# Attention and routed experts on one core: two buffers for the loads, an order from a repeating table of times, and dummy products at twelve places

## The chip, the cores and the metric

The kernel runs on one NeuronCore of a Trainium2 chip. The metric is the time of one execution in microseconds of device time. Before the change the median of three runs is 1302.24 us (1299.56 to 1303.64).

## The reference

```
# q, k, v: (8 batches, 8 heads, 1152, 64), float32
q_pool = q.reshape(B, H, 576, 2, D).mean(axis=3)
scores = (q_pool @ k^T) / 8;  scores -= max over keys
attn = exp(scores) / (sum + 1e-9);  out = attn @ v          # (8, 8, 576, 64)
x = out.transpose(0, 2, 1, 3).reshape(4608, 512)
logits = x @ w_gate                                          # 8 experts
# greedy: go through all logits from the largest; give a token to an expert
# while the token is free and the expert holds fewer than 576 tokens
out[tokens of e] = relu(x[tokens of e] @ w1[e]) @ w2[e]
```

## The kernel before, in words

**Stages.** `attention()` works through 64 heads as 32 pairs (n = 0 to 31), two heads s = 0 and 1 of a pair after each other. `experts()` follows; it assigns the tokens and runs eight feed-forward blocks. The change lies in `attention()` alone.

**A head.** 1152 keys are nine blocks of 128, 576 pooled queries are the moving side. A step g is one key block of one head; a pair has 18. For each step the scores of 288 queries at a time are two products (L600 with the high parts, L601 with the low parts and the maxima) into one of three PSUM banks `sc`; ScalarE takes the exponential into `P` (L604; ten buffers); POOL, in five or six of 18 steps DVE, subtracts the high half of `P` from `P` and keeps the rest in `PM` (L607; ten buffers); and TensorE adds 15 small products (L617) into `av`. These are issued in groups of one or two steps. After nine steps DVE divides `av` and writes `X` (L639): one such evacuation ends each half of a pair.

**What a pair needs before its first scores.** SP loads `QD`, `KD`, `VD` (L389, L392, L396), of each of which there is one buffer. DVE sums query pairs into `QS` (L401), ScalarE sums absolute values into `VJ` (L406 for keys, L415 for queries), a few tiny DVE operations (L419 to L425) make scales, ScalarE writes the high halves `KH` (L440) and `QH` (L429; DVE at L431 for pair 0), DVE the low halves `KL` and `QL` (L442, L432), and SP copies all of them to `KA`, `KB`, `QA`, `QB` (L450) and `BD` (L436), which have two buffers each. The row maxima of the scores are estimated a pair ahead: 27 products (L497; L505 and L501 for pair 0) into the two double banks `mt`, reduced by DVE (`MX`, L524; for pair 0 partly through `MS`, L539 and L541), turned by TensorE (L554, L570) and written into `QB` (L558 and L561 for pair 0, `AU` and a DMA, L575, otherwise). `V` is split likewise (L466, L480, L483). After every second pair the gate is applied (L658, L661, L672, L676 or L678), and `X` is stored (L721).

**The order.** Every operation is put into a list by `add` with an engine, an estimated duration, what it reads and writes, and a due time. `Order.emit` is a list scheduler: it plays the engines forward with those durations and, among operations that are ready, takes the one with the lowest due time plus a lead from the table `LEAD`. What it yields is only an order: each engine runs its own sequence, waiting on semaphores. Small DVE and POOL operations that build tables for the experts (`routing_tables`, L254 to L292) are items of the same list.

**Warm-up.** 50 products of `ones` (L728) stand at the head of TensorE's sequence, and 65 more (L730) between the products of pair 0.

Of the kernel before, what the change touches and what calls it, by code (L numbers as in the profile page):

```python
# [1433 lines left out]
```

## Time and profile before

| | us |
|---|---|
| median of three runs | 1302.24 |
| the profiled execution | 1307.96 |
| its span, first to last instruction | 1306.2 |
| busy in the span: PE | 1247.8 |
| DVE | 1038.2 |
| POOL | 777.7 |
| ACT | 769.9 |

The profiled execution is 1.76 us longer than its span and 5.72 us longer than the median of the runs. PE is TensorE's products, PEld its weight loads, ACT ScalarE, POOL GpSimd, SP the engine that issues most DMAs. The ends of products are modelled and overlap, so a full PE is not PE at its peak; what one product costs is read from the starts of its row and of the next. The clock column is the share of 2.4 GHz that TensorE was granted; it knows two levels, 1.0 and 0.5.

### The profile page before, as it was taken

The numbers are of one execution on the slowest core, as the hardware profiler recorded it, in microseconds if no ns is written. First come the engines' busy times: TensorE is split into PE (matmuls) and PEld (weight loads), VectorE is DVE, ScalarE is ACT, GpSimd is POOL, SyncE is SP. The second block draws the span as 40 slices with busy tenths as digits, with TensorE's granted clock in tenths as the row PEclk, the third lists the DMA queues.
The fourth block names the chain that finished last, engine by engine and source line by source line (L and its number), as shares of the span: only waits on it lengthen the run. The fifth ranks groups of instructions, "written<-read, shape, count | busy, mean of one in ns | idle before, by whom it ended". The sixth has DMA issues, their size and how long they took to land.

```text
span 1306.2 us, 39238 instructions
## 1 busy us (share of the span) xinstructions
PE 1247.8 (96%) x15419; PEld 1008.1 (77%) x15419; DVE 1038.2 (79%) x2606; ACT 769.9 (59%) x1901; POOL 777.7 (60%) x746
## 2 busy tenths in 40 slices
PE   7899999999999999999999997799999999999996
PEld 4577787777777777777777776587978889798895
DVE  8999999999999999899999985898876767752120
ACT  4588777877877877877877864143333324334330
POOL 5275576565656656656657563257667667586631
PEclk8799999999999999999999998999999999999998
DMA  4655555654654654654655520225445343454301
GB/s 150 154 167 144 156 151 139 174 148 126 186 145 121 178 147 117 177 150 119 181 149 140 126 60 20 66 102 197 170 133 150 130 126 124 151 172 143 125 14 37
DMA packets 123541, 175.25 MB, mean 134 GB/s; under 512 B 49500, under 2 KB 86364, under 8 KB 121180
## 3 DMA queue, kind: packets, MB, share of 16 engines
q1 hardware_dynamic: 114876, 120.29, 34.2%
q0 software_dynamic: 8336, 52.44, 11.5%
q8 instruction: 121, 1.98, 0.7%
q14 instruction: 64, 0.52, 0.1%
q10 hardware_dynamic: 144, 0.02, 0.0%
HBM read 99.63 MB, written 18.87 MB: 91 GB/s over the span
## 4 chain that ended last, share of the span: by engine, by line
PE 72%; DVE 16%; issue 5%; DMA 4%; ACT 1%; SPq 1%; POOL 0%; POOLq 0%; DVEq 0%; ACTq 0%
PE ph L1327 16%; PE av L617 14%; PE po L1357 13%; PE mt L497 8%; PE sc L600 8%; PE sc L601 7%; DVE MX L524 4%; DVE PM L607 4%; DMA KA<-KL 2%; DMA KD<-in_kt_dram 1%; PE mt L658 1%; PE po L1354 1%; DVE KL L442 1%; DMA QA<-QH 1%; PE rt L1001 1%
## 5 line engine op out<-in xcount | busy, mean ns | idle before, releaser
L607 POOL TENSOR_TENSOR PM<-P 128x576 f16<-128x576 f32 x413 | 473.4, 1174 | 312.4 <-ACT P L604 263.8
L604 ACT ACTIVATE P<-sc 128x288 f32<-128x288 f32 x1152 | 396.1, 413 | 162.7 <-PE sc L601 151.4
L524 DVE TENSOR_REDUCE MX<-mt 128x2 f32<-128x768 f32 (+1 forms) x443 | 399.4, 919 | 47.1 <-PE mt L497 43.8
L600 PE MATMUL sc<-QA,KA 128*128 128x288 f16 x1152 | 309.9, 286 | 10.9 <-ACT P L604 8.9
L617 PEld LDWEIGHTS <-P 128*128 128x128 bf16 x5760 | 297.5, 98 | 27.8 <-issue 0.7
L601 PE MATMUL sc<-QB,KB 66*128 66x288 f16 (+1 forms) x1152 | 311.7, 288 | 0.6 <-DMA QB<-AU 0.4
L617 PE MATMUL av<-V,P 128*128 128x65 f16 (+1 forms) x5760 | 306.0, 193 | 1.2 <-DVE V L483 1.2
L617 PE MATMUL av<-V,PM 128*128 128x65 f16 x2880 | 296.4, 195 | 0.0
L617 PEld LDWEIGHTS <-PM 128*128 128x128 f16 x2880 | 265.4, 97 | 1.3 <-issue 1.3
L497 PE MATMUL mt<-KH,BD 128*128 128x384 f16 x837 | 200.2, 326 | 3.4 <-DVE MX L524 1.6
L1357 PE MATMUL po<-W2H,HX 128*128 128x512 f32 x512 | 168.2, 399 | 0.0
L601 PEld LDWEIGHTS <-KB 66*128 66x128 f16 (+1 forms) x1152 | 112.0, 97 | 66.7 <-issue 29.6
L1327 PE MATMUL ph<-XH,W1H 128*128 128x320 f32 (+1 forms) x512 | 153.0, 299 | 1.0 <-issue 0.5
L1327 PE MATMUL ph<-XL,W1H 128*128 128x320 f32 (+1 forms) x512 | 152.4, 298 | 1.6 <-DVE XL L1226 1.5
L1327 PE MATMUL ph<-XH,W1L 128*128 128x320 f32 (+1 forms) x512 | 152.3, 298 | 1.0 <-issue 1.0
L600 PEld LDWEIGHTS <-KA 128*128 128x128 f16 x1152 | 112.9, 98 | 49.5 <-issue 15.7
L1332 ACT ACTIVATE HX<-ph 128x256 fp32r<-128x256 f32 (+1 forms) x128 | 51.5, 413 | 134.0 <-PE ph L1327 125.5
L607 DVE TENSOR_TENSOR PM<-P 128x576 f16<-128x576 f32 x163 | 123.5, 767 | 6.4 <-ACT P L604 5.5
L1357 PE MATMUL po<-W2L,HX 128*128 128x512 f32 (+1 forms) x320 | 127.6, 399 | 0.0
L1336 DVE SCALAR_TENSOR_TENSOR HX<-ph,HX 128x256 fp32r<-128x256 f32 x128 | 52.9, 415 | 81.1 <-ACT HX L1332 77.6
L1357 PEld LDWEIGHTS po<-W2H,HX 128*128 128x128 f32 x512 | 95.3, 189 | 18.5 <-issue 1.7
L497 PEld LDWEIGHTS <-BD 128*128 128x128 f16 x837 | 75.3, 98 | 30.8 <-issue 10.4
(233 smaller groups left out, 1899.7 us busy)
## 6 DMA issues: line engine op xcount, KB each, us to landing
QD<-in_qt_dram SPq DMA_DIRECT2D x32, 576.0 KB
KD<-in_kt_dram SPq DMA_DIRECT2D x64, 288.0 KB
VD<-in_v_dram SPq DMA_DIRECT2D x32, 576.0 KB
QA<-QH SPq DMA_DIRECT2D x128, 72.0 KB
KA<-KH SPq DMA_DIRECT2D x64, 144.0 KB
KB<-KH SPq DMA_DIRECT2D x64, 144.0 KB
KA<-KL SPq DMA_DIRECT2D x64, 144.0 KB
x_dram<-X SPq DMA_DIRECT2D x16, 576.0 KB
```

What stands on the lines that cost most here:

```text
L442: od.add(t + 5 + 2 * z, "DVE", 727, lock=1, fn=lambda h=h: nc.vector.scalar_tensor_tensor(KL[0][:, h], KD[0][:, h], sk, KH[i][:, h], op0=O ...
L497: nc.tensor.matmul(out, BD[i][:, j], KH[i][:, ks], start=True, stop=True)
L524: od.add(t, "DVE", d, lambda: nc.vector.tensor_reduce(dst, src, axis=AX.X, op=OP.max), r=[mk], w=[("MX", i, j, c) for j, c in what], tag=" ...
L600: nc.tensor.matmul(c[:, :288], KA[i][:, s, ks], QA[i][:, s, qs], start=True, stop=False)
L601: nc.tensor.matmul(c[:, :288], KB[i][:kr, s, ks], QB[i][:kr, s, qs], start=False, stop=True)
L604: od.add(g + 0.1 + 0.01 * t, "ACT", 293, lambda c=c, qs=qs: nc.scalar.activation(p[:, qs], c[:, :288], AF.Exp, scale=1.0 / UNIT), r=[ck], ...
L607: od.add(g + 0.2, en, dur, lock=1, fn=lambda: eng.tensor_tensor(pm, p, hi, op=OP.subtract), r=[("P32", g % NP, 0), ("P32", g % NP, 1)], w= ...
L617: nc.tensor.matmul(out, w[:, qs], v, start=kb == 0 and j == 0 and y == 0, stop=kb == NKB - 1 and y == 2, skip_group_check=True)
L1327: nc.tensor.matmul(p, a[:, d, fs], b[:, d, qs], start=z == 0, stop=z == 11)
L1332: nc.scalar.activation(HH[:, f, qs], p, AF.Relu)
L1336: V.scalar_tensor_tensor(HL[:, f, 64 + 256 * hf:320 + 256 * hf], p[:, :256], 0.0, h[:, :256], op0=OP.max, op1=OP.subtract)
L1357: nc.tensor.matmul(o[:n], a[:, z, q0:q0 + n], b[:, z], start=z == 0 and y == 0, stop=z == 7, skip_group_check=True)
```

## The change

Three things, all in `attention()`:

1. `KD`, `QD`, `VD` get two buffers each; a pair uses those of number n % 2.
2. The list scheduler's forward play gives way to `Timed.emit`: an item's key is n times 23600 plus a number from the table `TIME`, found by the pair's own prefix (pairs 0 to 3, the last two as y and z) or else by e or o for even and odd pairs, and by the operation's name and count. Items are emitted by lowest key among those whose predecessors have been emitted. No durations enter. Which engine does what is unchanged.
3. Ahead of twelve items of pairs 0 to 2 on TensorE, `FILL` puts 7 to 45 products of `ones` (185 in all), into columns 384 to 511 of the first bank of `mt`.

```diff
+class Timed(Order):
+    def when(self, i):
+        n, name, t = self.names[i]
+        if name is None:
+            return -1e6
+        for p in ("0123" + "-" * self.pairs)[n] + ("yz"[n - self.pairs + 2] if n + 2 >= self.pairs else "-") + "eo"[n % 2]:
+            if p + name in self.table:
+                return n * self.period + self.table[p + name]
+        return t / NSTEP * self.period + self.period
+    def emit(self):
...
+        while heap:
+            _, i = heapq.heappop(heap)
+            for _ in range(FILL.get("%d%s" % self.names[items[i]][:2], 0)):
+                self.fill()
+            self.items[items[i]][4]()
...
+PERIOD = 23600
+FILL = {"0mm0a": 45, "0mm1b": 24, "0mm0b": 7, "0mmf": 12, "0wv0a": 9, "0mmi": 9, "0mm0d": 13, "0augtb": 11,
+        "0qkb4a": 13, "2mm0a": 9, "2mm2a": 9, "2mm3a": 24}
+TIME = {"0auga": -30939, "0augb": -19565, "0augta": -16763, "0augtb": -11483, "0av0a10a": 8356, "0av0a12a": 11915,
...
-    od = Order(LEAD, LATE)
...
+    od = Timed(TIME, PERIOD, npair)
+    od.fill = lambda: nc.tensor.matmul(mt[0][:, 0, 384:], ones, ones, start=True, stop=True)
...
-    KD = several(1, [128, S], F32, "KD")
-    QD = several(1, [128, 2, M], F32, "QD")
-    VD = several(1, [128, 2, NKB, D], F32, "VD")
+    KD = several(2, [128, S], F32, "KD")
+    QD = several(2, [128, 2, M], F32, "QD")
+    VD = several(2, [128, 2, NKB, D], F32, "VD")
...
+            od.add(t, "SP", 1200, lambda h=h: nc.sync.dma_start(KD[n % 2][:, h], kt[n][:, h]), w=[("KD", n % 2, z)],
```

What it moves, at two places. The first is the head of DVE's sequence, from the high half of pair 0's queries (`QH`) on. Before (line numbers of before; `MX0` and `KH0` belong to pair 0; `KS`, `KE` are the scales; `mt` the banks of the maxima):

```order
L431 TENSOR_SCALAR QH0_81<-QS0_112,KS0_102 128x576
L432 SCALAR_TENSOR_TENSOR QL0_83<-QS0_112,KS0_102,QH0_81 128x576
L442 SCALAR_TENSOR_TENSOR KL0_80<-KD0_109,KS0_102,KH0_78 128x576
L524 TENSOR_REDUCE MX0_119<-mt0_149 128x2
L442 SCALAR_TENSOR_TENSOR KL0_80<-KD0_109,KS0_102,KH0_78 128x576
L524 TENSOR_REDUCE MX0_119<-mt1_150 128x2
L524 TENSOR_REDUCE MX0_119<-mt0_149 128x2
L401 TENSOR_TENSOR QS0_112<-QD0_110 128x576
L539 TENSOR_TENSOR MS_118<-MS_118 128x5x192
L524 TENSOR_REDUCE MX0_119<-mt1_150 128x2
L539 TENSOR_TENSOR MS_118<-MS_118 128x5x96
L524 TENSOR_REDUCE MX0_119<-mt0_149 128x2
```

With the change (the numbers of lines differ by the added code; L717 is `KL`, L706 `QH`, L707 `QL`, L676 `QS`, L799 `MX`, and what ends in 1 belongs to pair 1):

```order
L717 SCALAR_TENSOR_TENSOR KL0_80<-KD0_109,KS0_102,KH0_78 128x576 x2
L700 TENSOR_SCALAR KS0_102<-KS0_102 128x1
L706 TENSOR_SCALAR QH0_81<-QS0_115,KS0_102 128x576
L707 SCALAR_TENSOR_TENSOR QL0_83<-QS0_115,KS0_102,QH0_81 128x576
L676 TENSOR_TENSOR QS0_115<-QD1_112 128x576
L799 TENSOR_REDUCE MX0_122<-mt1_153 128x2
L694 TENSOR_SCALAR KE1_105<-KS1_103 128x1
L696 TENSOR_SCALAR KE1_105<-KS1_103,KE1_105 128x1
L698 TENSOR_SCALAR KS1_103<-KE1_105 128x1
L799 TENSOR_REDUCE MX0_122<-mt0_152 128x2
L700 TENSOR_SCALAR KS1_103<-KS1_103 128x1
L717 SCALAR_TENSOR_TENSOR KL0_80<-KD1_110,KS1_103,KH1_79 128x576 x2
```

Both `KL` of pair 0 now stand ahead of its `QH`, and the sums, scales and `KL` of pair 1 stand between the maxima of pair 0. On SP, likewise, the keys of pair 1 are loaded ahead of the second half of the keys of pair 0, and on DVE the second `ndiag` (L373 before), which waits for POOL's last fill, stands ahead of pair 0's scales. The tables for the experts, which DVE built between the maxima of pair 0 (L267 to L292), now stand in pair 2 of its sequence.

The second place is SP's queue in the middle of the program, at the load of an odd pair's keys (`KD`), which is issued some three pairs ahead of their scores. Before:

```order
L436 DMA BD0_92<-QH0_81 64x9x64 x2
L392 DMA KD0_109<-in_kt_dram 128x576 x2
L450 DMA KB0_86<-KH0_78 64x1152
L450 DMA KA0_84<-KL0_80 64x1152
L450 DMA QA0_88<-QH0_81 64x576
L450 DMA KA0_84<-KH0_78 64x1152
L450 DMA QA0_88<-QH0_81 64x576
```

With the change, the same load, now to the second buffer:

```order
L850 DMA QB0_90<-AU_101 1x9x64 x2
L667 DMA KD1_110<-in_kt_dram 128x576 x2
L725 DMA KB1_87<-KH1_79 64x1152
L725 DMA QA1_89<-QH1_82 64x576
L725 DMA KA1_85<-KL0_80 64x1152
L725 DMA QA1_89<-QH1_82 64x576
```

The load stood behind the store of `X` and the copies `BD` of a pair and had to wait until the one buffer was read; now it stands right behind the copies of the maxima (`AU`) of the pair under way and goes to the buffer that is not being read. On ScalarE, the sum over it (`VJ` from `KD`) stands in the same half of the even pairs as before; in the odd pairs it has moved from the seventh step to the last two.

## Rows read from the trace of the kernel before

**Rows 1.** Busy time in four stretches: from the start to the first evacuation, the pairs in their regular turn, the last pairs, the experts. Columns: stretch (us), its length, busy us (instructions) of PE, PEld, DVE, ACT, POOL, granted clock, DMA share, GB/s.

```profile
0.00:53.30 53.30, 40.50 (x361) 27.55 (x362) 45.66 (x113) 28.35 (x64) 20.91 (x36) 0.74 0.53 154
...
107.00:753.30 646.30, 636.09 (x10224) 500.16 (x10223) 604.31 (x1125) 506.59 (x1296) 400.47 (x353) 1.00 0.55 148
753.30:806.00 52.70, 51.28 (x896) 41.71 (x894) 34.79 (x63) 32.01 (x87) 32.90 (x33) 1.00 0.17 44
806.00:1306.20 500.20, 469.55 (x3169) 400.07 (x3169) 301.58 (x1215) 162.06 (x353) 291.14 (x299) 0.97 0.37 121
```

**Rows 2.** DVE in order of time, the evacuation that ends a pair's first half: of pairs 0, 2, 3, 4, then of 20, 21 and 29. Columns: start, duration, engine, line, operation.

```profile
53.28 0.48 DVE L639 TENSOR_TENSOR X<-av,RS 128x320 f32<-128x320 f32 x1
...
106.99 0.47 DVE L639 TENSOR_TENSOR X<-av,RS 128x320 f32<-128x320 f32 x1
130.32 0.48 DVE L639 TENSOR_TENSOR X<-av,RS 128x320 f32<-128x320 f32 x1
154.57 0.48 DVE L639 TENSOR_TENSOR X<-av,RS 128x320 f32<-128x320 f32 x1
...
538.23 0.48 DVE L639 TENSOR_TENSOR X<-av,RS 128x320 f32<-128x320 f32 x1
563.82 0.48 DVE L639 TENSOR_TENSOR X<-av,RS 128x320 f32<-128x320 f32 x1
...
753.29 0.47 DVE L639 TENSOR_TENSOR X<-av,RS 128x320 f32<-128x320 f32 x1
```

**Rows 3.** Who waited for whom between 107 and 753.3 us: total us, times, longest.

```profile
ACT VJ L406 <- DMA KD<-in_kt_dram: 8.5, 8, 1.8
...
PE sc L600 <- ACT P L604: 6.6, 8, 1.1
```

**Rows 4.** PE in order of time in the regular turn, at four places where products follow each other without a wait: maxima, 30 weighted sums, six scores; then the gate's transposes and its products.

```profile
396.51 0.81 PE L497 MATMUL mt<-KH,BD 128*128 128x384 f16 x4
397.16 0.22 PE L617 MATMUL av<-V,P 128*128 128x65 f16 x2
...
398.07 0.49 PE L497 MATMUL mt<-KH,BD 128*128 128x384 f16 x2
...
399.30 0.28 PE L600 MATMUL sc<-QA,KA 128*128 128x288 f16 x1
...
400.05 0.22 PE L617 MATMUL av<-V,P 128*128 128x65 f16 x2
...
430.58 0.82 PE L658 MATMUL mt<-ident,X 128*128 128x128 f32 x6
...
437.84 0.83 PE L672 MATMUL mt<-XT,wgs 128*8 128x384 f32 x6
```

**Rows 5.** Busy time in three stretches of 5 us near the start, columns as in rows 1.

```profile
30.00:35.00 5.00, 2.42 (x11) 1.59 (x11) 4.00 (x15) 1.57 (x4) 1.45 (x3) 0.57 0.00 0
35.00:40.00 5.00, 3.15 (x12) 1.31 (x11) 4.93 (x12) 3.88 (x8) 0.89 (x1) 0.50 0.39 68
40.00:45.00 5.00, 3.76 (x47) 2.91 (x46) 4.97 (x7) 1.88 (x5) 0.00 (x0) 0.50 0.94 284
```

**Rows 6.** PE in order of time near the start: the first product of pair 0, a run of dummy products, and the last wait before the clock falls. In brackets: idle time before, and what ended it.

```profile
10.71 0.82 PE L505 MATMUL mt<-KH,QH 64*128 64x384 f16 x2 [3.61 <-DVE QH L431]
...
20.08 2.17 PE L730 MATMUL av<-ones 128*128 128x128 bf16 x33
...
32.58 0.16 PE L469 MATMUL mt<-VM,ones 128*128 128x1 bf16 x1 [3.63 <-DVE MX L524]
```

**Rows 7.** DVE in order of time near the start: the halves of queries and keys, maxima, a fold, the first `QB`, and one of the tables for the experts.

```profile
9.23 1.43 DVE L431 TENSOR_SCALAR QH<-QS,KS 128x576 f16<-128x576 f32 x1
10.69 0.82 DVE L432 SCALAR_TENSOR_TENSOR QL<-QS,KS,QH 128x576 f16<-128x576 f32 x1
11.43 0.81 DVE L442 SCALAR_TENSOR_TENSOR KL<-KD,KS,KH 128x576 f16<-128x576 f32 x1
...
13.75 1.81 DVE L524 TENSOR_REDUCE MX<-mt 128x2 f32<-128x768 f32 x2
...
16.15 0.65 DVE L539 TENSOR_TENSOR MS<-MS 128x960 bf16<-128x960 bf16 x1
...
22.41 0.69 DVE L558 SCALAR_TENSOR_TENSOR QB<-mt,ndiag 9x512 f16<-9x512 f32 x1 [1.27 <-PE mt L554]
...
26.54 1.80 DVE L276 TENSOR_SCALAR nib<-scratch 128x16 f32<-128x16 int32 x2
```

**Rows 8.** POOL in order of time: the last of the fills at the start.

```profile
10.40 0.38 POOL L364 MEMSET V<- 128x18 f16 x1
```

**Rows 9.** DVE's groups between 107 and 753.3 us that read two operands from SBUF, largest first: xcount, busy us, mean ns, idle before.

```profile
L607 DVE TENSOR_TENSOR PM<-P 128x576 f16<-128x576 f32 x135 | 100.6, 754 | 0.4
L483 DVE SCALAR_TENSOR_TENSOR V<-VD,VS,V 128x576 f16<-128x576 f32 x54 | 43.8, 810 | 0.0
L442 DVE SCALAR_TENSOR_TENSOR KL<-KD,KS,KH 128x576 f16<-128x576 f32 x54 | 41.8, 813 | 0.8 <-DMA QA<-QH 0.8
L432 DVE SCALAR_TENSOR_TENSOR QL<-QS,KS,QH 128x576 f16<-128x576 f32 x27 | 21.8, 807 | 0.0
L401 DVE TENSOR_TENSOR QS<-QD 128x576 f32<-128x576 f32 x26 | 19.5, 749 | 0.0
```

**Rows 10.** POOL's one group in the same stretch, columns as in rows 9.

```profile
L607 POOL TENSOR_TENSOR PM<-P 128x576 f16<-128x576 f32 x353 | 402.2, 1168 | 249.7 <-ACT P L604 204.7 <-issue 44.3 <-DVE RS L645 0.2
```

More of the change, by code (lines that the diff above doesn't have):

```diff
@@ L1 @@
+import heapq
 import math
@@ L158, in emit, with __init__, add @@
             items[i][4]()
+class Timed(Order):
+    def __init__(self, table, period, pairs):
+        Order.__init__(self)
+        self.table, self.period, self.pairs = table, period, pairs
+        self.pair, self.names, self.seen = 0, [], {}
+    def add(self, t, eng, dur, fn, r=(), w=(), late=0, first=0, tag=None, kind=0, lock=None, k=None):
+        Order.add(self, t, eng, dur, fn, r, w, late, first, tag, kind, lock)
+        name = ("pm" if tag in ("pmP", "pmD") else tag or "o") + ("" if k is None else str(k))
+        z = self.seen[self.pair, name] = self.seen.get((self.pair, name), -1) + 1
+        self.names.append((self.pair, name + "abcdefghijklmnopqrstuvwxyz"[z] if z < 26 else None, t))
+    def when(self, i):
[7 more added lines that the diff above has]
+    def emit(self):
+        items = sorted(range(len(self.items)), key=lambda i: (self.items[i][0], i))
+        writer, readers, n = {}, {}, len(items)
+        need = [set() for _ in range(n)]
+        for i, j in enumerate(items):
+            _, _, _, _, _, r, w, _, _ = self.items[j]
+            for k in r:
+                if k in writer:
+                    need[i].add(writer[k])
+                readers.setdefault(k, []).append(i)
+            for k in w:
+                if k in writer:
+                    need[i].add(writer[k])
+                need[i].update(readers.get(k, ()))
+                readers[k] = []
+                writer[k] = i
+            need[i].discard(i)
+        users, left = [[] for _ in range(n)], [len(x) for x in need]
+        for i, x in enumerate(need):
+            for j in x:
+                users[j].append(i)
+        heap = [(self.when(items[i]), i) for i in range(n) if not left[i]]
+        heapq.heapify(heap)
+        done = 0
+        while heap:
[3 more added lines that the diff above has]
+            self.items[items[i]][4]()
+            done += 1
+            for j in users[i]:
+                left[j] -= 1
+                if not left[j]:
+                    heapq.heappush(heap, (self.when(items[j]), j))
+        assert done == n
@@ L165 @@
       0.5093, "grp": [2, 4, 6, 8, 9]}
-LEAD = {"0aug": -2.8, "0augt": -46.4, "0expa": 0.1, "0expa.0": 46.8, "0expa.1": 10.0, "0expa.10": -32.7,
[54 rows of a table removed]
-LATE = {"0aug": 450, "0augt": -200, "0expa": -200, "0expb": -100, "0fold": 150, "0ka": 300, "0kh": 800,
[9 rows of a table removed]
+PERIOD = 23600
+FILL = {"0mm0a": 45, "0mm1b": 24, "0mm0b": 7, "0mmf": 12, "0wv0a": 9, "0mmi": 9, "0mm0d": 13, "0augtb": 11,
+        "0qkb4a": 13, "2mm0a": 9, "2mm2a": 9, "2mm3a": 24}
+TIME = {"0auga": -30939, "0augb": -19565, "0augta": -16763, "0augtb": -11483, "0av0a10a": 8356, "0av0a12a": 11915,
[161 rows of a table added]
+        "ekl0a": -52439, "ekl1a": -50101, "eksa": -52153, "eksb": -42505, "eksc": -39168, "eksd": -53094,
[19 rows of a table added]
+        "evsd": -14025, "exa": -15498, "exb": -20318, "oauga": -1401, "oaugda": -35130, "oaugdb": -33276,
[9 rows of a table added]
+        "ogcb": 2554, "ogla": -47730, "ogma": 39737, "ogpa": -45501, "ogta": 20686, "ogtb": 34983, "okaa": -55857,
+        "okh0a": -59827, "okh1a": -59832, "okl0a": -45452, "okl1a": -45762, "oksa": -53093, "oksb": -47552,
+        "oksc": -60791, "oksd": -46190, "olk0a": -75548, "olk1a": -75143, "olqa": -72386, "olva": -37173,
[14 rows of a table added]
+        "oqla": -31091, "oqsa": -55621, "orc0a": -47731, "orc1a": -45803, "orca": -46658, "orcb": -46657,
[3 rows of a table added]
+        "ovsa": -8962, "ovsb": -47547, "ovsc": -1253, "ovsd": -45742, "oxa": -45741, "oxb": -41122,
+        "yauga": -13339, "yaugda": -34688, "yaugdb": -34086, "yaugta": -5700, "yav0a10a": 20470, "yav0a12a": 23549,
[29 rows of a table added]
+        "yvsc": -14869, "yvsd": -14831, "yxa": -15559, "yxb": -23182, "zauga": -6260, "zaugda": -36021,
[10 rows of a table added]
+        "zgcc": -4293, "zgla": -48199, "zglb": -10685, "zglc": -4861, "zgma": 29730, "zgmb": -1071, "zgmc": -3502,
+        "zgta": 21940, "zgtb": 33019, "zgtc": -1945, "zkaa": -55873, "zkh0a": -62597, "zkh1a": -64471,
+        "zkl0a": -46228, "zkl1a": -46049, "zksa": -51839, "zksb": -48519, "zksc": -60167, "zksd": -47096,
[19 rows of a table added]
+        "zvsc": -2259, "zvsd": -45994, "zxa": -46710, "zxb": -45546}
 def routing_tables(nc, pool, ident, jp, scratch, do):
@@ L388, in load @@
     def load(n, t):
-        od.add(t, "SP", 2440, lambda: nc.sync.dma_start(QD[0], qt[n]), w=["QD"], late=2000, tag="lq")
+        od.add(t, "SP", 2440, lambda: nc.sync.dma_start(QD[n % 2], qt[n]), w=[("QD", n % 2)], late=2000, tag="lq")
         for z in range(2):
             h = slice(z * M, z * M + M)
-            od.add(t, "SP", 1200, lambda h=h: nc.sync.dma_start(KD[0][:, h], kt[n][:, h]), w=[("KD", z)],
+            od.add(t, "SP", 1200, lambda h=h: nc.sync.dma_start(KD[n % 2][:, h], kt[n][:, h]), w=[("KD", n % 2, z)],
                    late=2000, tag="lk", k=z)
     def load_v(n, t):
-        od.add(t, "SP", 2500, lambda: nc.sync.dma_start(VD[0], v[n]), w=["VD"], late=2500, tag="lv")
+        od.add(t, "SP", 2500, lambda: nc.sync.dma_start(VD[n % 2], v[n]), w=[("VD", n % 2)], late=2500, tag="lv")
     def split(n, t):
         i = n % 2
-        od.add(t, "DVE", 666, lock=1, fn=lambda: nc.vector.tensor_tensor(QS[0], QD[0][:, 0], QD[0][:, 1], op=OP.add),
-               r=["QD"], w=["QS"], tag="qs")
+        od.add(t, "DVE", 666, lock=1, fn=lambda: nc.vector.tensor_tensor(QS[0], QD[n % 2][:, 0], QD[n % 2][:, 1], op=OP.add),
+               r=[("QD", n % 2)], w=["QS"], tag="qs")
         if n:
-            od.add(t + .5, "ACT", 1150, lambda: nc.scalar.activation(VJ, KD[0], AF.Abs, accum_out=KS[i][:, 0:1]),
-                   r=[("KD", 0), ("KD", 1)], w=[("KN", i)], tag="ka")
+            od.add(t + .5, "ACT", 1150, lambda: nc.scalar.activation(VJ, KD[n % 2], AF.Abs, accum_out=KS[i][:, 0:1]),
+                   r=[("KD", n % 2, 0), ("KD", n % 2, 1)], w=[("KN", i)], tag="ka")
         else:
@@ L439, in split @@
             h = slice(z * M, z * M + M)
-            od.add(t + 4 + 2 * z, "ACT", 670, lambda h=h: nc.scalar.activation(KH[i][:, h], KD[0][:, h], AF.Copy, scale=sk),
-                   r=[("KD", z), ("SK", i)], w=[("KH", i, z)], tag="kh", k=z)
+            od.add(t + 4 + 2 * z, "ACT", 670, lambda h=h: nc.scalar.activation(KH[i][:, h], KD[n % 2][:, h], AF.Copy, scale=sk),
+                   r=[("KD", n % 2, z), ("SK", i)], w=[("KH", i, z)], tag="kh", k=z)
             od.add(t + 5 + 2 * z, "DVE", 727, lock=1, fn=lambda h=h: nc.vector.scalar_tensor_tensor(
-                KL[0][:, h], KD[0][:, h], sk, KH[i][:, h], op0=OP.mult, op1=OP.subtract),
-                r=[("KD", z), ("SK", i), ("KH", i, z)], w=[("KL", z)], tag="kl", k=z)
+                KL[0][:, h], KD[n % 2][:, h], sk, KH[i][:, h], op0=OP.mult, op1=OP.subtract),
+                r=[("KD", n % 2, z), ("SK", i), ("KH", i, z)], w=[("KL", z)], tag="kl", k=z)
     def spread(n, t):
@@ L464, in values @@
         i = n % 2
-        flat = VD[0].rearrange("p s k d -> p (s k d)")
+        flat = VD[n % 2].rearrange("p s k d -> p (s k d)")
         od.add(t, "ACT", 1150, lambda: nc.scalar.activation(VJ, flat, AF.Abs, accum_out=VM[i]),
-               r=["VD"], w=[("VM", i)], tag="vabs")
+               r=[("VD", n % 2)], w=[("VM", i)], tag="vabs")
         od.add(t + AT["vs"] - 1, "PE", 30, lambda: nc.tensor.matmul(mt[0][:, 0, :1], ones, VM[i].bitcast(BF)[:, 1:2], start=True, stop=True),
@@ L480, in values @@
             od.add(t + AT["vh"] - 1 + AT["vd"] * s, "ACT", 670, lambda s=s: nc.scalar.activation(
-                V16[i][:, s, :, D:2 * D], VD[0][:, s], AF.Copy, scale=VS[i]),
-                r=["VD", ("VS", i)], w=[("VH", i, s)], tag="vh", k=s)
+                V16[i][:, s, :, D:2 * D], VD[n % 2][:, s], AF.Copy, scale=VS[i]),
+                r=[("VD", n % 2), ("VS", i)], w=[("VH", i, s)], tag="vh", k=s)
             od.add(t + AT["vh"] + AT["vd"] * s, "DVE", 727, lock=1, fn=lambda s=s: nc.vector.scalar_tensor_tensor(
-                V16[i][:, s, :, 0:D], VD[0][:, s], VS[i], V16[i][:, s, :, D:2 * D], op0=OP.mult, op1=OP.subtract),
-                r=["VD", ("VS", i), ("VH", i, s)], w=[("VL", i, s)], tag="vl", k=s)
+                V16[i][:, s, :, 0:D], VD[n % 2][:, s], VS[i], V16[i][:, s, :, D:2 * D], op0=OP.mult, op1=OP.subtract),
+                r=[("VD", n % 2), ("VS", i), ("VH", i, s)], w=[("VL", i, s)], tag="vl", k=s)
     def needs(n, what):
@@ L726, in attention @@
     od.cur = None
-    for _ in range(AT["wu"]):
-        od.add(-70, "PE", 60, lambda: nc.tensor.matmul(mt[0][:, 0, :128], ones, ones, start=True, stop=True), w=["m0"])
-    for _ in range(AT["wv"]):
+    for z in range(AT["wu"]):
+        od.add(-70, "PE", 60, lambda: nc.tensor.matmul(mt[0][:, 0, :128], ones, ones, start=True, stop=True), w=["m0"], tag="wu", k=z)
+    for z in range(AT["wv"]):
         od.add(-42, "PE", 54, lambda: nc.tensor.matmul(av[:, :128], ones, ones, start=True, stop=True),
-               r=[("CM", 0, 0)], w=["av"], first=-1)
+               r=[("CM", 0, 0)], w=["av"], tag="wv", k=z)
     for i in range(2):
@@ L736, in attention @@
         base = NSTEP * (n - 1)
-        od.cur = n
+        od.cur = od.pair = n
         if n == 0:
@@ L776, in attention @@
     for g in range(npair * NSTEP):
-        od.cur = g // NSTEP
+        od.cur = od.pair = g // NSTEP
         step(g)
     for n in range(1, npair, 2):
-        od.cur = None
+        od.cur, od.pair = None, n
         g = NSTEP * n + NSTEP
@@ L793, in attention @@
         store(n, g + LAG + 1)
-    od.cur = None
+    od.cur, od.pair = None, 2
     C = routing_tables(nc, top, ident, jp, scratch,
-                       lambda eng, dur, fn: od.add(2 * NSTEP, eng, dur, fn, w=["tables"]))
+                       lambda eng, dur, fn: od.add(2 * NSTEP, eng, dur, fn, w=["tables"], tag="tables"))
     od.emit()
```

6 lines of the change are left out of this document (2 added, 4 removed), and 327 rows, old and new, of tables (LATE, LEAD, TIME).

## The prediction

> **What bounds the kernel now.** First the stages [rows 1]. From 107.00 to 753.30 us 27 pairs take 646.30 us, 23.94 each, with PE busy for 636.09, DVE for 604.31 and POOL for 400.47: three engines near their ends, PE first. The experts take 500.20 us with the same code in the same order, and I leave them. The start is worse than the turn: the first half pair ends at 53.28 us and pair 2's first half at 106.99 [rows 2], 53.71 us for two pairs, where two pairs later on take 47.58 (106.99 to 154.57).
>
> Second, how even the turn is. From an odd pair to the next even one took 24.25 us (130.32 to 154.57). From an even pair to the odd one it took 23.33 after pair 2, but 25.59 after pair 20 [rows 2]. Something not fixed by the order lengthens some pairs, and the waits name a candidate: ScalarE stands 8.5 us, in eight waits, for the load of `KD` before it sums absolute values, and TensorE's scores stand 6.6 us, in eight waits also, for exponentials [rows 3], which lie behind that sum in ScalarE's sequence. So a late load holds a sum, the sum holds exponentials, these hold the scores' banks, and PE stops.
>
> Third, what PE would need if it never waited, from the starts of neighbouring rows [rows 4]: 30 weighted sums (two steps) from 397.16 to 398.07, 0.91, so nine times that, 8.19 a pair; six score products from 399.30 to 400.05, 0.125 each, 72 of them 9.0; four maxima from 396.51 to 397.16, 0.1625 each, 27 of them 4.39; the gate, once in two pairs, nine transposes (1.5 times 0.82) and 0.83, 1.03 a pair. Sum 22.6. So 1.3 us a pair, 36 in all, is loss, of which late loads are 8.5.
>
> Fourth, the clock: between 30 and 45 us it is 0.57, 0.50 and 0.50 [rows 5], the 1.2 GHz level, and PE was idle for 3.63 us until 32.58, shortly before it is seen low [rows 6].
>
> **The change part by part.**
>
> *Two buffers for loads.* No bytes are added. The load of keys goes out as soon as SP reaches it, and no longer after the last reader of the one buffer. ScalarE's waits of 8.5 us [rows 3] should go; in the odd pairs the sum has also moved ten steps later, over half a pair after the load. Bounds: 0 (other work would have hidden the waits) and 10 (what the uneven pairs show: 25.59 against 23.33 is 2.3 in one). I take 8.5, since the uneven pairs say these waits reach PE. Late next are the copies to `KA` and `KB`, used most of a pair later.
>
> *The order in the turn.* The engines have the same instructions per pair, in nearly the same places; on PE a few weighted sums and maxima change sides. No row prices that. The upper bound is the remaining loss, 36 less 8.5, some 27; below nothing it could lose as much as a new wait costs (a rival, below). I take 5: idle PE in the turn is 646.30 less 636.09, 10.2 [rows 1], most of it the late loads', so the rest hides between products where an order can find little.
>
> *The start.* Here the order changes most. The second `ndiag` now stands ahead of the scales on DVE and waits for POOL's last fill, which ends at 10.78 [rows 8]. A shift of the fills among themselves does not alter that sum. With two conversions, ScalarE's `KH` and two `KL` (0.81 each) behind it, `QH` ends at some 15 us, not 10.66 [rows 7], and the first product comes some 4.5 us later than 10.71 [rows 6]. From there to the first `QB` DVE has, by durations [rows 7]: two `QL` 1.6, two `QS` (as `QL` at most) 1.6, seven maxima at 0.9, 6.3, two `KL` of pair 1 1.6, six folds and reductions at 0.65 at most, 3.9, and 1.27 for the transpose: 16.3, and less where rows overlap. So the first `QB` comes at some 31 us, where it came at 22.41: 8.5 later. The second half of pair 0 needs two more maxima and a second `QB`, at some 35 us. What comes back: pair 1 is by then split, and the tables for the experts (as 1.80 for two `nib` [rows 7]), some 6 us of DVE between 23.5 and 33.3, are out of the way. From there to the first evacuation DVE has some 18 operations, five `PM`, seven maxima, two `V`, one `KL`, one `QL` and small ones, 13.5 us at the durations above. The first evacuation then falls at 48.6, 4.7 earlier than 53.28. After it two pairs need no less than the 47.6 of the regular turn plus the tables' some 4 us, 51.6 against 53.7: 2.1 more. I take 6.8, say 7. Bounds: 11 gained if the tables are free in pair 2, 8.5 lost if the late first `QB` is not made good.
>
> *Dummy products.* 185, at 0.066 each when PE takes them back to back (33 in 2.17 [rows 6]) 12 us, in twelve places. I cost them at nothing: the first 45 fill the 3.61 us wait for `QH` [rows 6], now longer, the rest stand before products that wait for DVE. If a cover is gone, its run of 7 to 24 delays PE by up to 1.6 us. They have a return if the clock stays at 1.0: between 35 and 45 us PE was busy for only 6.91 us [rows 5], at the low level half of that is loss, 3.5 at most, and I count it within the start, where DVE (9.90 busy of 10) sets the pace.
>
> *The end.* Pairs 30 and 31 have no next pairs to prepare; the stretch of 52.70 us holds 51.28 of PE [rows 1]. Nothing, at most 1.4.
>
> **Sum.** Against the profiled execution's 1307.96: less 8.5, 5 and 7 is 1287.5. It stood 5.72 over the median of the runs, and I keep that distance: **1282**. A difference of 0.3% is about what can be told from no change.
>
> One rule speaks against more. In the turn DVE's operations on two SBUF operands are busy for 227.5 us (100.6, 43.8, 41.8, 21.8, 19.5 [rows 9]) and POOL for 402.2 [rows 10], 629.7 of 646.3 together. If they exclude each other, 16.6 us are free. The Trainium skill's page "SBUF — State Buffer", section "Who interferes with whom", says just that: a DVE instruction with two SBUF inputs and a GpSimd instruction that reads SBUF block each other, and the first holds the shared interface to its end. By it the turn could give at most 16.6 us and no order could pass 23.3 us a pair; my 13.5 would stand. No row read here shows the exclusion itself.
>
> **The rivals.**
>
> *The port is the bound.* If the two engines' 629.7 us are kept apart, and handing over takes the 16.6 that is left, the turn gives nothing, and late loads only fill gaps it had anyway. For it: a sum of 97%. Against it: pairs differ by 2.3 us [rows 2] with the same DVE and POOL work. The start's 7 alone gives 1295.
>
> *The start is not made good.* The first `QB` is 8.5 late, DVE has the tables in pair 2, where it is 94% busy [rows 1], and nothing returns: plus 8.5 at the start, less 8.5 for the loads, nothing from the order, 1302. Here the dummies too fail to do what they are for.
>
> *A new wait in every pair: slower.* In odd pairs the weighted sums of steps 2 and 3 now stand on PE behind the scores of step 12, which they stood ahead of by several products. `P` has ten buffers, so the exponentials of step 12 overwrite those of step 2 and must wait for these sums; the next scores in their bank wait for the exponentials. The longest such wait before is 1.1 us [rows 3]. At 1.1 in each of 29 pairs, 32, less 7 and 8.5, it is 1302 plus 16.5, 1319. It decides from 0.53 a pair. Against it: the sums of two groups stand there together, 1.8 us in which ScalarE catches up.
>
> **How the numbers follow.** My forecast 0.64 (its own range 1266 to 1294: start 3 to 11, order 0 to 15, loads 5 to 10), the port 0.13, the start 0.12, the new wait 0.11. Faster 0.77, the same 0.12, slower 0.11. The range goes from 1264 to 1303: it takes in the first two rivals and leaves out the slow one and some of my own lower end.
>
> **What would show it.** Right: no ScalarE wait for `KD` in the turn; even to odd pairs all near 23; two pairs in about 47; the first evacuation before 50 us and pair 2's near 100; the clock at 1.0 between 30 and 45 us. The first product later than 14 us. Wrong: scores waiting for exponentials more than 6.6 us in the turn, DVE short of 604 us of work there but the pairs as long, or the first evacuation after 55.

## The result and the profile after: slower by 0.8%

The median of six runs is **1312.91 us** (1311.10 to 1314.72), against 1301.30 of six runs of the kernel before: 11.6 us slower. The ratio on record is 1.0078 (interval 1.0058 to 1.0098); the quotient of the two medians is 1.0089. The forecast was 1282, with a range from 1264 to 1303. The profiled execution took 1314.72, its span is 1312.9.

Where the time went shows in the evacuations that end a pair's first half, of pairs 0 to 4 and 29 (DVE: start, duration, line, operation), as in [rows 2]:

```profile
59.09 0.49 DVE L914 TENSOR_TENSOR X<-av,RS 128x320 f32<-128x320 f32 x1
91.22 0.49 DVE L914 TENSOR_TENSOR X<-av,RS 128x320 f32<-128x320 f32 x1
120.31 0.49 DVE L914 TENSOR_TENSOR X<-av,RS 128x320 f32<-128x320 f32 x1
144.86 0.49 DVE L914 TENSOR_TENSOR X<-av,RS 128x320 f32<-128x320 f32 x1
169.59 0.49 DVE L914 TENSOR_TENSOR X<-av,RS 128x320 f32<-128x320 f32 x1
...
764.28 0.49 DVE L914 TENSOR_TENSOR X<-av,RS 128x320 f32<-128x320 f32 x1
```

Pair 2's stands at 120.31, not at 106.99 [rows 2]: 13.3 us are lost by then, 5.8 up to the first evacuation and 7.5 in the two pairs behind it. From there 27 pairs take 643.97, not 646.30: 2.3 come back. So the whole loss lies in the first 120 us, where the forecast had a gain of 7.

The stages (columns as in rows 1):

```profile
0.00:59.09 59.09, 45.01 (x507) 33.92 (x508) 39.39 (x89) 31.22 (x68) 20.26 (x27) 0.83 0.55 161
59.09:120.31 61.22, 53.87 (x816) 40.88 (x814) 57.74 (x117) 41.70 (x103) 34.43 (x39) 1.00 0.46 121
120.31:764.33 644.02, 632.43 (x10226) 499.59 (x10225) 618.12 (x1127) 516.47 (x1293) 406.15 (x352) 1.00 0.56 149
764.33:813.00 48.67, 48.15 (x878) 39.68 (x877) 36.09 (x56) 31.62 (x85) 31.33 (x32) 1.00 0.13 33
813.00:1312.90 499.90, 469.52 (x3185) 400.64 (x3184) 305.00 (x1220) 165.02 (x355) 290.79 (x299) 0.98 0.37 121
```

DVE is busy for 39.39 of the first 59.09 us (45.66 of 53.30 in [rows 1]): there it had time to spare and waited.

A second execution of the kernel before was profiled (e7, one run, 1300.84 us), with no edit.

> The kernel before once more, for a second profiled execution. If the waits for KD are the same in each execution, the turn from pair 2 to pair 29 is 646 us again and the pairs that are longer than 24.25 and 22.93 are the same ones; if they come by chance, they are other pairs and the sum differs by some us.

```profile
50.54 0.48 DVE L639 TENSOR_TENSOR X<-av,RS 128x320 f32<-128x320 f32 x1
79.99 0.48 DVE L639 TENSOR_TENSOR X<-av,RS 128x320 f32<-128x320 f32 x1
104.26 0.48 DVE L639 TENSOR_TENSOR X<-av,RS 128x320 f32<-128x320 f32 x1
...
753.78 0.48 DVE L639 TENSOR_TENSOR X<-av,RS 128x320 f32<-128x320 f32 x1
```

It reaches pair 2 at 104.26, 2.7 earlier than the first, and its turn takes 649.52, 3.2 more; ScalarE waits 8.7 us for `KD` there, in nine waits. The sum of the waits is nearly the same. The 2.7 us lie ahead of the first evacuation, at 50.54; in e5, e9 and e15 below, whose order up to there is the same, it stands at 50.81, 50.61 and 50.51. So 53.28 [rows 2] was late in that one execution. Its experts take 495.5 us (803.5 to 1299.0), those of the first 503.1 (803.1 to 1306.2): judged by this execution, the distance of the first to its median lay mostly in unchanged code. Against this execution the change loses 16.0 up to pair 2 and gains 5.6 in the turn.

### The profile page after: what moved, and what is told of

It is laid out like the page before. It is cut to its first block, busy times and chain, and to the rows that moved or that the text cites. A ratio compares the mean times of both kernels' runs of the same rounds, so it can differ in the third digit from the quotient of the medians.

```text
span 1312.9 us, 39481 instructions
## 1 busy us (share of the span) xinstructions
PE 1249.0 (95%) x15604; PEld 1014.7 (77%) x15604; DVE 1056.3 (80%) x2606; ACT 786.0 (60%) x1901; POOL 783.0 (60%) x746
## 4 chain that ended last, share of the span: by engine, by line
PE 74%; DVE 16%; issue 5%; DMA 2%; ACT 1%; POOL 1%; SPq 0%; DVEq 0%; POOLq 0%; ACTq 0%
PE ph L1602 16%; PE av L892 14%; PE po L1632 13%; PE mt L772 9%; PE sc L875 8%; PE sc L876 8%; DVE MX L799 5%; DVE PM L882 3%; DVE KL L717 2%; PE po L1629 1%; DMA KA<-KL 1%; PE rt L1276 1%; PE mt L933 1%; DVE QS L676 1%; PE mt L578 1%
## 5 line engine op out<-in xcount | busy, mean ns | idle before, releaser
L882 POOL TENSOR_TENSOR PM<-P 128x576 f16<-128x576 f32 x413 | 479.3, 1185 | 316.3 <-ACT P L879 305.5
L879 ACT ACTIVATE P<-sc 128x288 f32<-128x288 f32 x1152 | 404.1, 411 | 138.3 <-PE sc L876 122.9
L799 DVE TENSOR_REDUCE MX<-mt 128x2 f32<-128x768 f32 (+1 forms) x443 | 393.0, 923 | 29.7 <-PE mt L772 16.2
L892 PEld LDWEIGHTS <-P 128*128 128x128 bf16 x5760 | 288.1, 98 | 23.1 <-issue 2.6
L892 PE MATMUL av<-V,P 128*128 128x65 f16 (+1 forms) x5760 | 296.0, 192 | 1.6 <-issue 1.4
L892 PE MATMUL av<-V,PM 128*128 128x65 f16 x2880 | 288.6, 194 | 0.0
```

The source lines that it names most:

```text
L799: od.add(t, "DVE", d, lambda: nc.vector.tensor_reduce(dst, src, axis=AX.X, op=OP.max), r=[mk], w=[("MX", i, j, c) for j, c in what], tag=" ...
L879: od.add(g + 0.1 + 0.01 * t, "ACT", 293, lambda c=c, qs=qs: nc.scalar.activation(p[:, qs], c[:, :288], AF.Exp, scale=1.0 / UNIT), r=[ck], ...
L882: od.add(g + 0.2, en, dur, lock=1, fn=lambda: eng.tensor_tensor(pm, p, hi, op=OP.subtract), r=[("P32", g % NP, 0), ("P32", g % NP, 1)], w= ...
L892: nc.tensor.matmul(out, w[:, qs], v, start=kb == 0 and j == 0 and y == 0, stop=kb == NKB - 1 and y == 2, skip_group_check=True)
```

## The experiments

Ratios are to the kernel before on the same chip, with their intervals; times in us can't be compared between chips, since the kernel before took 1301.20 to 1302.77 on three of them and 1308.35 on that of e13 to e16. Line numbers differ from kernel to kernel. "Without dummies" means without the change's 185; those of the kernel before stay.

**The dummies (e1).**

```
-FILL = {"0mm0a": 45, "0mm1b": 24, ...}
+FILL = {}
```

> The change without its 185 dummy products, everything else in the same order. Theory A (the dummies stand in the chain of the start): they write a part of the first maxima bank, wait for the DVE reduction of that bank, and the next real product and the next reduction wait for them. In the trace of the change the runs before 45.7 us that follow such a wait take 2.72, 0.56, 0.84, 0.68, 0.66, 1.55, 1.33 and 1.09 us, 9.4 in all, of which the first (2.72) and those before the transposes are surely in the chain. Then 4 to 9 us less than the change: 1304 to 1309, the first evacuation at 50 to 55 us in place of 59.1. Theory B (the order of the start is slow by itself, the dummies are covered): within 1.5 us of 1312.9, first evacuation 58 to 60. Theory C (the dummies hold the clock up and pay for themselves): 2 to 5 us slower than the change, with the clock below 1.0 for longer than its 10 to 15, 15 to 25 and 35 to 47 us.

1307.67 us, 1.0035 (1.0018 to 1.0052), against the change's 1.0078: theory A. The first evacuation comes at 53.40, pair 2's at 114.24, 6.1 earlier than with dummies. PE at the start of the change (start, duration; in brackets idle time before, and what ended it):

```profile
14.81 1.46 PE L780 MATMUL mt<-KH,QH 64*128 64x384 f16 x4 [5.77 <-DVE QH L706]
18.76 2.72 PE L578 MATMUL mt<-ones 128*128 128x128 bf16 x24 [2.49 <-DVE KS L700]
21.41 0.82 PE L780 MATMUL mt<-KH,QH 64*128 64x384 f16 x2
```

DVE beside it, the second reduction and the third:

```profile
17.76 0.95 DVE L799 TENSOR_REDUCE MX<-mt 128x2 f32<-128x768 f32 x1
...
22.26 0.96 DVE L799 TENSOR_REDUCE MX<-mt 128x2 f32<-128x768 f32 x1 [2.03 <-PE mt L780]
```

Without dummies the same product and reductions, of PE and of DVE:

```profile
17.32 0.80 PE L779 MATMUL mt<-KH,QH 64*128 64x384 f16 x2 [1.05 <-DVE KE L693]
```

```profile
20.14 1.81 DVE L798 TENSOR_REDUCE MX<-mt 128x2 f32<-128x768 f32 x2
```

The 24 dummies write an unused part of `mt[0]`, and so wait until the second reduction, from 17.76 to 18.71, has read that bank (the row names `KS`, a tiny operation that DVE runs right behind it); the next product, whose bank had been free since 17.27, stands behind them and starts at 21.41, not at 17.32. DVE then waits 2.03 us for it, and this reduction comes 2.1 us later than without dummies. The rest of the loss comes from the later runs of dummies, which are not taken apart here. The dummies do lift the clock, and the balance is a loss. With them (25 to 35 us, columns as in rows 1):

```profile
25.00:30.00 5.00, 3.92 (x36) 2.13 (x36) 3.58 (x5) 2.26 (x7) 0.00 (x0) 1.00 0.83 190
30.00:35.00 5.00, 3.83 (x64) 3.51 (x63) 4.39 (x13) 4.86 (x9) 0.00 (x0) 1.00 0.92 250
```

Without them:

```profile
25.00:30.00 5.00, 4.25 (x34) 3.35 (x34) 4.53 (x11) 3.45 (x8) 0.00 (x0) 0.50 0.73 161
30.00:35.00 5.00, 4.08 (x46) 3.41 (x44) 2.11 (x7) 2.48 (x6) 0.00 (x0) 0.88 0.82 186
```

At 0.50 from 15 to 30 us, the 1.2 GHz level, the first evacuation still comes 5.7 us sooner. No kernel here has the higher clock without the dummies that wait, so what the clock alone is worth there is not shown.

**The first 45 dummies alone (e16).**

```
-FILL = {"0mm0a": 45, "0mm1b": 24, ...}
+FILL = {"0mm0a": 45}
```

> The change with the first 45 dummies alone (ahead of the first product, where no reduction waits for them). If only dummies that stand between a reduction and the next product of its bank cost time, this is the change without dummies: within 1.5 us of 1307.7, first evacuation at 53.4. If the first 45 cost too: 1309 or more. If they pay by a higher clock: 1305 or less.

1.0057 (1.0036 to 1.0077), which overlaps both e1's interval and the change's; in the trace the evacuations of pairs 0 and 2 stand at 53.14 and 113.85, as in e1. These 45 neither cost nor give anything at the start; the whole time is too rough to say more.

**Two buffers alone (e2, e5).** e2, from the kernel before (`QD` and `VD` likewise):

```
-KD = several(1, [128, S], F32, "KD")
+KD = several(2, [128, S], F32, "KD")
-nc.sync.dma_start(KD[0][:, h], kt[n][:, h])
+nc.sync.dma_start(KD[n % 2][:, h], kt[n][:, h])
```

> The kernel before with nothing but two buffers each for KD, QD and VD, under its own list scheduler. The prediction's step (late loads cost the turn 8.5 us): 8.5 us less than before, 1293, pairs even at 24.25 and 22.93. Rival (the waits for loads are hidden by other engines, or the list scheduler meets other waits): within 3 us of 1301.3.

1395.51 us, 1.0711 (1.0674 to 1.0749). It doesn't answer the question: the list scheduler was run without its offsets per step and wrote another order. With e5, below, it shows what order alone is worth here: the same instructions, 93 us more than the 1302.77 of the kernel before on that chip. In e5 the order is the old one, instruction by instruction on every queue (the code in short):

```
def rank(self):                  # list scheduler, with the old kernel's keys
    ...  ("QD", b) -> "QD";  ("KD", b, z) -> ("KD", z);  ("VD", b) -> "VD"
for i in rank(): items[i][4]()   # tiles KD[n % 2], QD[n % 2], VD[n % 2]
```

> Exactly the order of the kernel before on every engine and queue, and only two buffers each for KD, QD and VD (the second kernel of the group before was to be this, but its list scheduler was run without the offsets it has per step, so that it wrote another order). The prediction's step (late loads cost the turn 8.5 us): 8.5 us less than before, about 1293; no ScalarE wait for KD; pairs at 24.25 and 22.93 throughout. Rival 1 (the loads were late by chance in the one profiled run, which stood 5.7 above the median): 1296 to 1300. Rival 2 (hidden by other engines): within 1.5 us of 1301.3.

1301.98 us, 0.9999 (0.9983 to 1.0015): rival 2, nothing, and the waits are still there. ScalarE's waits in the turn:

```profile
ACT VJ L771 <- DMA KD<-in_kt_dram: 6.4, 8, 2.6
```

One of them, SP's queue first:

```profile
439.96 0.46 SPq L815 DMA_DIRECT2D KB<-KH  x1
440.46 1.64 SPq L815 DMA_DIRECT2D KA<-KL  x1
442.15 0.60 SPq L815 DMA_DIRECT2D QA<-QH  x1
442.85 1.56 SPq L940 DMA_DIRECT2D QB<-AU  x2
444.45 0.53 SPq L815 DMA_DIRECT2D QB<-QL  x1
445.08 2.68 SPq L801 DMA_DIRECT2D BD<-QH  x2
447.81 1.12 SPq L757 DMA_DIRECT2D KD<-in_kt_dram  x2
```

and ScalarE:

```profile
453.00 1.16 ACT L771 ACTIVATE VJ<-KD 128x1152 bf16<-128x1152 f32 x1 [2.59 <-DMA KD<-in_kt_dram]
```

The load has a free buffer, but it stands in SP's queue behind eight copies. The first, to `KB`, goes out at 439.96, after 3.7 us in which SP waits for the scores that still read its target; the eight keep SP until 447.81. The load itself then holds the chain of this stretch, the work that ended last, followed back:

```profile
448.48 4.41 DMA KD<-in_kt_dram
```

Behind it in that chain stand `VJ`, an exponential and scores. The pair around this wait took 27.2 us (evacuations at 438.2 and 465.4) in place of 22.9, so such waits do reach PE. What SP waits for in the turn of e5 (170.4 in the same row of the kernel before):

```profile
SPq L815 <- PE sc L966: 166.2, 40, 6.0
```

In the change ScalarE has no wait for `KD` in the turn: the table puts the load long before the sum (at 432.39 and 449.80 for one pair).

**The tables for the experts (e6).** In e1, all twelve rows moved from pair 2 to pair 31:

```
-"2tablesa": -6078, ...
+"2tablesa": 678322, ...          # + 29 * 23600
```

> The change without dummies, and with the tables for the experts moved from pair 2 to pair 31, where DVE has time. Theory (DVE is full in pair 2, so the tables' 4 to 5 us there lengthen it one for one): pair 1 to pair 2 takes 24.3 in place of 29.09, the whole 1307.7 less 4 to 5, 1303, if the last pairs hide the tables. Rival (the pairs of the start are bound by PE or by products that wait, the tables fill gaps): within 1.5 us of 1307.7.

1306.78 us, 1.0047 (1.0027 to 1.0067): the rival. Pair 1 to pair 2 takes 27.84 (84.75 to 112.59), 1.25 less than 29.09; the last pairs, from 756.30 to 806.7, take 1.6 more.

**Whose order is it (e3, e4, e9, e13 to e15).** The old order up to the first scores of pair CUT, the table's behind, two buffers, no dummies:

```
early = rank()[:index of (CUT, "qka0a")]
for i in walk(lambda i: (0, place in early) if i in early else (1, place in the table's order)): ...
```

e3 (CUT 3) and e4 (its mirror: the table's start, the list scheduler's turn) had the same fault as e2.

> Two buffers for loads; all that the list scheduler of the kernel before puts ahead of the first scores of pair 3 stands in that order, the rest in the order of the table of times; no dummies. Theory 1 (the change loses at the start, 13.3 us to the evacuation of pair 2, and gains 2.3 in the turn): the change less 13.3, 1299 to 1300, with evacuations at 53.3 and about 107 and the turn's 24.58 and 22.88. Theory 2 (the start's loss comes back partly whatever the start is, because the turn is bound elsewhere and absorbs it): 1305 to 1309.

1313.72 us, 1.0073 (1.0048 to 1.0099).

> The mirror image: two buffers, the table's order and the dummies up to the first scores of pair 3, the list scheduler's order behind them. Theory 1 (start and turn add up): first evacuation at 59.1, that of pair 2 at 120.3, then the turn of the second kernel of this group; so the time of that kernel plus 13, 1306 to 1316. Theory 2 (the list scheduler makes good what the start lost): less than 1305.

1413.63 us, 1.0848 (1.0813 to 1.0884). e3 lacked the old start (its first evacuation stood at 58.06) and e4 the old turn, so nothing follows from them. With the true old order, CUT 4:

> Two buffers, no dummies; up to the first scores of pair 4 exactly the order of the kernel before, behind them the table's order. (The third kernel of the first group was meant as this, but had another order at its start, for the reason given with the frozen order.) Theory 1 (the table's start is a poor order and its turn a better one, the two add up): evacuations at 50 to 53 and 104 to 107, then the table's 24.58 and 22.88 with few longer pairs, 1301.5 less some 4, 1296 to 1299, faster than both kernels. Theory 2 (the table's turn prepares odd pairs nearly a pair earlier than the order before did; that work has to be done once more than the start can hold, so whoever enters this turn pays for it): one pair near the change of orders takes 28 to 32 in place of 24.3, and the whole 1301 to 1306.

1297.68 us, **0.9968 (0.9951 to 0.9985)**: theory 1, a little faster than both kernels. Evacuations of pairs 0, 2, 3, 4 and 29:

```profile
50.61 0.48 DVE L1004 TENSOR_TENSOR X<-av,RS 128x320 f32<-128x320 f32 x1
...
104.40 0.47 DVE L1004 TENSOR_TENSOR X<-av,RS 128x320 f32<-128x320 f32 x1
127.32 0.47 DVE L1004 TENSOR_TENSOR X<-av,RS 128x320 f32<-128x320 f32 x1
153.60 0.49 DVE L1004 TENSOR_TENSOR X<-av,RS 128x320 f32<-128x320 f32 x1
...
747.29 0.49 DVE L1004 TENSOR_TENSOR X<-av,RS 128x320 f32<-128x320 f32 x1
```

The turn is entered at a cost of 1.7 (26.28 in place of 24.58) and then keeps its pace. CUT 1, 2 and 3:

> As the version that keeps the order of the kernel before up to pair 4, but only up to the first scores of pair 1. If what the table does ahead of pair 1 costs the 10 us that lie between that version (1297.7) and the change without dummies (1307.7), this one is at 1297 to 1300; if it is the table's order within pairs 1 and 2, it is at 1304 to 1309, with pair 1 to pair 2 at 27 to 30.

1.0046 (1.0026 to 1.0066); 36.56 from pair 0 to 1, 27.84 from 1 to 2.

> The same up to the first scores of pair 2. If the table's order within pair 1 costs most: 1297 to 1300; if that within pair 2 does, or entering the turn there: 1301 to 1307.

1.0028 (1.0006 to 1.0050); 29.46, then 28.92 from pair 1 to 2 (80.73 to 109.65), with the tables for the experts in their old place.

> The same up to the first scores of pair 3. If the turn can be entered at an odd pair as well as at an even one: within 2 us of 1297.7; if entering it there leaves work undone that the table has ahead: 1300 or more, with one pair of 27 or more.

0.9978 (0.9958 to 0.9998); 24.25 from pair 1 to 2, 24.33 from 2 to 3. So the table's order of pair 2 costs 3.6 to 4.7 us (27.84 and 28.92 against 24.25), whichever order leads into it. In CUT 2 the change of orders falls into that interval too; e6, with the table's order all through, has the same 27.84 as CUT 1. Entered at pair 3 or 4, the table's order costs no more than some 2 us of entering: pair 4 is reached at 153.29 and 153.60, in e7 at 151.56. Between e1 and CUT 4 the 9.8 us up to pair 2 divide into 2.8 up to the first evacuation (53.40, 50.61), 2.2 up to pair 1's (31.75, 29.53) and 4.8 up to pair 2's (29.09, 24.26), of which the tables are 1.25.

**Rows 2 and 3 struck out (e10).** In e1:

```
-"2...": ..., "3...": ...,        # all but "2tables..."
```

> The change without dummies, with the table's own rows for pairs 2 and 3 struck out (but those of the tables for the experts), so that these two pairs follow the rows of the regular turn. If the special rows of pairs 2 and 3 are what makes pair 1 to pair 2 take 29.09, it falls towards 25 to 27 and the whole to 1303 to 1306; if it is the entry into the turn itself, it stays at 28 to 30 and the whole within 1.5 us of 1307.7, or worse.

1330.79 us, 1.0226 (1.0195 to 1.0257); 38.23 from pair 0 to 1 and 44.85 from 1 to 2. The regular rows can't serve there; the special rows are poor, but better than none.

**What bounds the turn (e8, e11, e12).** In e1, from pair 4 on, three separate kernels:

```
-src = m[:, :, :384]                                   # e8, DVE
+src = m[:, :, :384 if n < 4 else 192]
-parts = ((a, hh, high), (a[:, :D], hh, low), (a, mm, high))   # e11, PE
+parts = (...)[:3 if n < 4 else 2]
-eng.tensor_tensor(pm, p, hi, op=OP.subtract)          # e12, POOL
+u = slice(0, M if en == "DVE" or n < 4 else M // 2)
+eng.tensor_tensor(pm[:, u], p[:, u], hi[:, u], op=OP.subtract)
```

> The change without dummies; from pair 4 on the maxima of two blocks are taken over half of the keys (192 of 384), which leaves part of the keys out of the estimate. It takes about 0.4 us from each of 13 operations, 5 us of DVE in a pair, and nothing from TensorE, POOL or the operations on two SBUF operands. Theory P (TensorE's products set the pace, 22.2 to 22.6 us of them a pair): two pairs stay at 47.46 less at most 1. Theory D (DVE's own time sets it, 45.2 of 47.46 by starts of neighbouring rows): two pairs fall by 2 us or more, to the next bound. Theory S (POOL and the DVE operations on two SBUF operands exclude each other and set it together): stays at 47.46.

> The change without dummies; from pair 4 on the products of V with the low part PM are left out (5 of 15 per step, 90 a pair, 0.03 us each, 2.7 us of PE a pair), DVE, ScalarE and POOL do the same work. Theory P (PE sets the pace): two pairs fall from 47.46 by 2 us or more, up to 5.4. Theory S (the two-operand work of DVE and POOL sets it): by less than 1. Theory M (no single engine: all are near their ends and each waits for the others in turn): 1 to 2, as the 0.9 that less DVE gave.

> The change without dummies; from pair 4 on POOL's PM is written for half of the queries only (288 of 576), which takes some 0.55 us from each of 12.5 POOL operations in a pair, 6.9 us of POOL and of the time in which DVE's operations on two SBUF operands are shut out. Theory S: two pairs fall by 2 us or more. Theory P: by less than 1. Theory M: 1 to 2.

From odd to even and from even to odd pair, by the most frequent interval: e1 24.58 and 22.88, together 47.46; less DVE 24.07 and 22.50, 46.57; less PE 24.19 and 23.64, 47.83; less POOL 24.99 and 22.87, 47.86. 9.3 us less of DVE's reductions in two pairs (271.7 to 169.5 in the some 22 pairs between 215 and 740 us) bring 0.89, 5.4 less of PE (180 products, at the 0.03 of the expectation) and 11 less of POOL nothing. Each was executed once: 1297.57, 1307.62 and 1317.53 us. With less DVE, DVE waits for PE (between 215 and 740 us; 13.0 in e1):

```profile
DVE MX L798 <- PE mt L771: 73.5, 117, 1.7
```

With less PE, PE waits for DVE (in e1 only the second row, 5.0):

```profile
PE mt L844 <- DVE CM L821: 19.2, 10, 1.9
PE mt L771 <- DVE MX L798: 11.9, 41, 0.6
```

The last two are not clean. What is taken away shifts the engines against each other, and operations of DVE on two SBUF operands then meet POOL's. `QL` in e11 and `KL` in e12 (shortest, median and longest in ns):

```profile
L706 DVE SCALAR_TENSOR_TENSOR QL<-QS,KS,QH x22: 807/1252/1700, 232.9 to 730.9; 128x576 f16<-128x576 f32 x22
```

```profile
L716 DVE SCALAR_TENSOR_TENSOR KL<-KD,KS,KH x44: 804/812/1224, 217.4 to 734.0; 128x576 f16<-128x576 f32 x44
```

In e1 both take 0.81. In e11 `QL` takes 1.70 between an even and an odd pair, and that interval is 0.76 longer; the other, with no such meeting, is 0.39 shorter. In e12 one of the four `KL` in two pairs takes 1.22, between an odd and an even pair, and that interval is 0.41 longer, the other unchanged.

So theory M is nearest, though the 1 to 2 us that it expected came in neither of the two: in e12 0.41 more of DVE lengthens the pairs by 0.41, and with 9.3 less of it PE stops them 0.89 lower. DVE is in front and PE within 1 us of it in two pairs, and in a fixed order work taken from one is waited for at the other. Theory S falls as a bound of the sums; single meetings of the two engines cost all the same.

## Why the prediction was wrong, point by point

*Two buffers, less 8.5: wrong.* The rows read were right, waits for `KD` do hold PE, but the step "The load of keys goes out as soon as SP reaches it" stopped there: it never asked when SP reaches it. Two buffers alone gave 0.9999 and left 6.4 of 8.5 us of waits. With the load earlier in SP's order, in the change, they are gone. Whether the table's order would do with one buffer was not tried.

*The order in the turn, less 5: right in sign together with the loads, too large.* Loads and order were to give 13.5; the turn is 2.3 shorter than in one execution of before and 5.6 shorter than in the other. Over all traces it takes 646.3 to 649.5 in the old order (before, e7, e5) and 642.7 to 645.9 where the table's order holds from pair 4 on at the latest (the change, e1, e6, e9, e13 to e16). The longer pairs are mostly gone, but the pace itself is 47.46 for two pairs where the old order keeps 47.18 when nothing waits: 24.25 [rows 2] and 22.93, from pair 4 (154.57) to pair 5. The bound of 27, PE's products alone at 22.6 a pair, was not within reach: DVE stood in front, and even with 9.3 us less of it e8's two pairs took 46.57, not 45.2.

*The start, less 7: wrong by 20, and this decides.* The forecast's first product (15 us) came at 14.81. Its first `QB` was to come at 31: it came at 35.02, and without dummies at 32.85. The first evacuation was to come at 48.6: 59.09, without dummies 53.40. Its base was late by 2.7, as e7 shows. Three terms failed. Dummies were costed at nothing since they "stand before products that wait for DVE"; they themselves wait for DVE, at another bank, and cost 6.1 up to pair 2. The count of DVE's operations up to the first evacuation left no time for waits: in e1 DVE waits 5.0 us for PE's products and transposes and 0.5 for ScalarE between 14 and 53.4 us, and the count was 4.8 short. And for the two pairs behind it the base was the regular turn, 47.6, with 4 for the tables; they took 60.8 without dummies. The tables were worth 1.25 of it, the order of pairs 1 and 2 the rest. What within that order holds pair 2 stays open; with the tables away (e6), DVE waits 3.6 us for maxima there and PE 1.8 for exponentials, which names the engines and not the row.

*Clock: half right.* It is 1.0 between 25 and 35 us and 0.58 and 0.50 after, not 1.0 until 45.

*The end:* 48.9 us from 764.28 to the last evacuation at 813.15, where before took 49.8. Right.

*The rivals.* "The start is not made good" named the place, but with 8.5 back from the loads (1302). "A new wait in every pair" would have given a slower kernel for a reason that isn't there: scores wait for exponentials 0.4 us in the turn after, 6.6 before [rows 3]. "The port is the bound" falls with e12. That the two engines do exclude each other shows in rows that the forecast lacked. POOL and DVE at one place of the turn after:

```profile
233.36 1.14 POOL L882 TENSOR_TENSOR PM<-P 128x576 f16<-128x576 f32 x1
237.23 2.88 POOL L882 TENSOR_TENSOR PM<-P 128x576 f16<-128x576 f32 x2 [2.73 <-ACT P L879]
```

```profile
237.18 0.81 DVE L707 SCALAR_TENSOR_TENSOR QL<-QS,KS,QH 128x576 f16<-128x576 f32 x1
```

A POOL operation takes 1.14; the one that starts beside DVE's `QL` takes 1.74 (2.88 less 1.14). The Trainium skill's page "SBUF — State Buffer", section "Who interferes with whom", says that such a pair of instructions blocks; the trace agrees, and in e8, where DVE's operations fell at other times against POOL's, so do DVE's `QS` and `QL`, which took 0.975 and 0.941 us on average there and 0.744 and 0.810 in e1. But a port that is full by sums, 97%, did not set the pace: with 11 us less of POOL in two pairs they were no shorter. What counts is where two operations meet: `QL` and `KL` in e11 and e12.

## What to carry to other kernels

A transfer that comes late may be held by its queue and not by its buffer: look at what stands ahead of it on the issuing engine before a second buffer is costed as a gain. Dummy work was free here where nobody waited on its tile (e16) and cost up to 6.1 us where another engine read the bank it wrote. A test that takes work from one engine shifts the others against each other: look for operations that got longer before its result is believed. When an order is replaced, price the start, where no engine is full, by the chain of waits between engines rather than by one engine's sum, and take the old order's own time for those pairs as the base; a new order may be used only where it is better (0.9968 with the old order up to pair 4 and the new one behind).
